# A recurrent mixer with a gated block: eight units' preparation laid over six columns, two of them in idle partitions and moved by transfers

## The chip, the cores and the metric

One core of one Trainium2 chip. The metric is the device time in microseconds (us) of one launch. Inputs are laid out on the host, all arithmetic is on the chip.

## The reference

A linear recurrence over 768 tokens for 4 batches of 8 heads with 40 features each, then a gated feed-forward block over the 4 batches. Cut to what matters:

```python
for t in range(S):
    y[:, :, t] = np.einsum('bhd,bhde->bhe', rt, state)
    Sa = np.einsum('bhde,bhe->bhd', state, at)
    state_decay = state * wt[:, :, None, :] - np.einsum('bhd,bhe->bhde', Sa, bt)
    state = state_decay + np.einsum('bhd,bhe->bhde', vt, kt)
# x = y of all heads side by side
h = np.maximum(x @ w_in, 0.0)
u, v = h[..., :512], h[..., 512:]
v_n = (v - mean(v)) / sqrt(var(v) + 1e-6)
v_s = np.einsum('ts,bsd->btd', w_spatial, v_n) + b_spatial[None, :, None]
out = (u * v_s) @ w_out
```

## The kernel before

**Layout.** `phase1` runs the recurrence in 24 chunks of 64 tokens (12 chunks for each of two pairs of batches). A chunk has 8 units (2 batches x 4 head pairs). A unit's two heads lie in the two halves of the 128 partitions (`par` 0 and 1). Of the 64 partitions of a half, 40 hold the head's features (E = 40); 24 hold padding. Tokens run along the free axis.

**Preparation** of a chunk q (needed some chunks later) is DVE's: `scan1` (L292) makes S, the products of the decay w from the end of the chunk backwards, and a reciprocal (L296); `scan2` (L301) makes Et, the forward products; `at_mul` (L318) and `sl_mul` (L324) make `at` (a times Et) and `sl` (b and k times S). The inputs of a chunk are one tile `ein` of 528 + 1536 elements per partition, two buffers, loaded by `prep_piece` (L279) in six transfers of 16 rows. `scr_store` (L312) sends the chunk's total decay out to memory, `scn_load` (L534) brings it back spread over the partitions. `lprime` (L339) makes the 32 x 32 diagonal blocks L' of the chunk's triangle on PE; `lblock` (L349) copies them with a mask into `Lc` on DVE. For every four chunks `invert` (L357 to L374) inverts the 32 x 32 triangles of `Lc` on DVE, in 30 steps of a product (L363) and a sum (L367) between transposes.

**The chunk loop** (chunk s) is a chain: `c_bp` (PE, L545; ACT copies it, L555), `c_ff` (L563; L571), `c_xx` (L581; L592), `c_mp` (L613, L619; DVE makes the state Mc, L630) and `c_y` (L641; DVE makes y, L654), then bp of s + 1. Beside it run the steps that make a later chunk's operands: `b_copy` (a copy of `at` into `At`, L392), `b_lka`, `b_h`, `b_tok`, `b_l21`, `b_zt`, `b_x21`, with copies on ACT and POOL's `strict` (L406). The feed-forward's first part (`m_*`) is woven in from chunk 11 on; `phase2` (L102) is the spatial product and the output projection.

**What sets the order.** Each engine, and SP's queue of transfers, does its instructions in program order. That order is the sorted list `plan`: `at(t, fn, ...)` gives each step a time t in units of chunks. `PREP` gives t of the preparation of a chunk q (scan1 at t + 0.20, the pieces of chunk q + 2 from t + 0.40, `lprime` at t + `LPO`), by default q - 8 + 0.01. All transfers but a few at the start are issued by SP.

Of the kernel before, what the change touches and what calls it, by code (L numbers as in the profile page):

```python
# [18 lines left out]
P = 128  # L19
C = 64  # L20
# [8 lines left out]
EW = WF + 3 * NU * C  # L29
NR = C + E  # L30
# [187 lines left out]
def phase1(ctx, tc, early, late, vtok, win, xs, vns, uts, dscr):  # L218
# [12 lines left out]
    fifo = [pool(f"fifo{i}") for i in range(GS)]  # L231
# [4 lines left out]
    etp = pool("etp", 9)  # L236
# [15 lines left out]
    ein = [p.tile([P, EW], F32, name=f"ein{i}") for i, p in enumerate((pin, pin, extra, extra))]  # L252
# [16 lines left out]

    def prep_load(s, rows, cols=slice(0, EW), i=None, queues=(nc.sync, nc.sync)):  # L270
        t = ein[s % 2 if i is None else i]
        for par in range(2):
            o = par * 64
            queues[par].dma_start(out=t[o:o + rows, cols], in_=early[par, s, 0:rows, cols])

    def prep_piece(s, k):
        par, r = k % 2, k // 2 * 16
        o = par * 64 + r
        nc.sync.dma_start(out=ein[s % 2][o:o + 16], in_=early[par, s, r:r + 16])  # L279

    def scan1(s, i=None):
        t = ein[s % 2 if i is None else i]
        Et = etp.tile([P, WF], F32, name="Et")
        at = fifo[s % 8].tile([P, NU, C], F32, name="at")
        sl = fifo[s % 8].tile([P, NU, 2, C], F32, name="sl")
        wseg = t[:, 0:WF]
        oth = t[:, WF:].rearrange("p (q n c) -> p n q c", q=3, c=C)
        sx = pin.tile([P, WF], F32, name="S", bufs=2)
        sv = sx.rearrange("p (n c) -> p n c", c=WSEG)
        st["pre", s] = (Et, at, sl)  # L290
        st["raw", s] = (wseg, oth, sv)
        nc.vector.tensor_tensor_scan(  # L292
            out=sx[:, ::-1], data0=wseg[:, ::-1], data1=ends[:, ::-1],
            initial=0.0, op0=ALU.mult, op1=ALU.add,
        )
        nc.vector.reciprocal(out=eseg[:, :, 0:1], in_=sv[:, :, 1:2])  # L296

    def scan2(s):
        Et, at, sl = st["pre", s]
        wseg, oth, sv = st["raw", s]  # L300
        nc.vector.tensor_tensor_scan(  # L301
            out=Et, data0=wseg, data1=ends, initial=0.0, op0=ALU.mult, op1=ALU.add,
        )
# [10 lines left out]
    def at_mul(s, eng, ns=slice(0, NU)):  # L314
        Et, at, sl = st["pre", s]
        oth = st["raw", s][1]
        Ev = Et.rearrange("p (n c) -> p n c", c=WSEG)
        eng.tensor_tensor(out=at[:, ns], in0=oth[:, ns, 0], in1=Ev[:, ns, 0:C], op=ALU.mult)  # L318

    def sl_mul(s, eng, ns=slice(0, NU)):  # L320
        Et, at, sl = st["pre", s]
        wseg, oth, sv = st["raw", s]
# [6 lines left out]
    def lprime(s, units=range(NU)):  # L329
# [4 lines left out]
        for n in units:  # L334
            for blk in range(2):
                for par in range(2):
# [3 lines left out]
                        pl[o:o + HB, n, :], lhsT=sl[PR[par], n, par, cs], rhs=at[PR[par], n, cs],  # L340
# [3 lines left out]
    def lblock(s):  # L344
        if s % GS == 0:
# [3 lines left out]
        nc.vector.tensor_tensor(  # L349
            out=Lc[:, u0:u0 + NU, :], in0=st.pop(("pl", s)),  # L350
            in1=maskl.unsqueeze(1).broadcast_to([P, NU, HB]), op=ALU.mult,
        )
# [33 lines left out]
    def b_copy(s, par):  # L386
        if par == 0:
            At = [jat.tile([P, NU, C], F32, name=f"At{i}") for i in range(2)]
            tk = jit.tile([P, NU, 2, E], F32, name="tk")
            st["blk", s] = (At, Rts[s % 2], tk, xfs[s % 2])  # L390
        at = st["pre", s][1]
        nc.sync.dma_start(out=st["blk", s][0][par][PR[par]], in_=at[PR[par]])  # L392
# [18 lines left out]
    def b_lka_out(s, par):  # L411
# [174 lines left out]
    def c_xx_out(s, g):  # L586
# [439 lines left out]
```

## Time and profile before

| | |
|---|---|
| median of 3 runs | 667.58 us (663.11 to 670.05) |
| profiled execution, its own time | 665.08 us |
| its span, first to last instruction | 663.3 us |
| mean granted TensorE clock | 0.943 |
| DVE busy | 448.4 us (68%) |
| PE busy | 571.8 us (86%) |
| ACT, POOL busy | 384.2 us, 225.9 us |
| transfers of SP's queue | 105672 packets, 84.31 MB |

The span is what the profile's tables cover; the execution's own time is 1.8 us more. Busy time leaves out waiting and the issue of transfers: SP's work is seen in its timeline alone. Stages differ, so busy time is read by windows. In a row of a timeline the bracket gives the idle time before it and what ended it; q behind an engine's name means its queue.

### The profile page before, as it was taken

How to read it: one execution, taken by the hardware profiler on the slowest of the kernel's cores; microseconds unless marked ns; L12 is line 12 of the kernel's file. 1: busy time of each engine (PE TensorE's matmuls, PEld its weight loads, DVE VectorE, ACT ScalarE, POOL GpSimd, SP SyncE). 2: the span in 40 equal slices, each digit the busy share in tenths (PEclk: the TensorE clock that was granted, in tenths of full speed). 3: DMA queues.
4: the chain of work that ended last, by engine and by line, in shares of the span. 5: the costliest groups of instructions: out<-in, count | busy, mean ns of one | idle time of the engine just before them, and what ended most of it. 6: DMA issues, size and time to landing. Idle time of an engine off the chain costs nothing.

```text
span 663.3 us, 25848 instructions
## 1 busy us (share of the span) xinstructions
PE 571.8 (86%) x10960; PEld 518.3 (78%) x10960; DVE 448.4 (68%) x970; ACT 384.2 (58%) x860; POOL 225.9 (34%) x298
## 2 busy tenths in 40 slices
PE   1447885498777887999999999999989999999997
PEld 1437674487766776888888888888878999999997
DVE  8999789989999999488896677343384842332220
ACT  2135662377666775688878887888765543221212
POOL 6013330224332334144341332332354843352221
PEclk9967997789787898999999999999998999999999
DMA  8654778477555546657565365375395557150001
GB/s 199 121 107 67 134 152 147 70 175 155 135 127 115 131 117 120 142 127 172 154 190 148 86 173 144 90 198 132 89 262 182 162 155 240 61 157 31 31 31 59
DMA packets 106331, 87.68 MB, mean 132 GB/s; under 512 B 35496, under 2 KB 92072, under 8 KB 104296
## 3 DMA queue, kind: packets, MB, share of 16 engines
q1 hardware_dynamic: 105672, 84.31, 52.0%
q10 hardware_dynamic: 544, 1.72, 1.2%
q8 instruction: 86, 1.41, 1.0%
q14 instruction: 29, 0.24, 0.1%
HBM read 59.20 MB, written 20.50 MB: 120 GB/s over the span
## 4 chain that ended last, share of the span: by engine, by line
PE 63%; DVE 15%; DMA 7%; issue 6%; ACT 4%; SPq 3%; POOL 1%; DVEq 0%; ACTq 0%; POOLq 0%
PE po L199 6%; PE pv L759 6%; PE pv L712 6%; PE pg L179 5%; PE pg L180 5%; PE pg L181 5%; PE ch L563 4%; PE bp L545 4%; PE ch L581 4%; PE bk L429 2%; DMA ein<-in_early 2%; DVE itmp L363 2%; PE bk L451 2%; PE bk L399 2%; PE bp L641 2%
## 5 line engine op out<-in xcount | busy, mean ns | idle before, releaser
L406 POOL TENSOR_SCALAR_AFFINE_SELECT Rt<-Rt 64x512 f32<-64x512 f32 (+1 forms) x144 | 83.8, 584 | 156.2 <-ACT Rt L592 128.5
L406 POOL TENSOR_SCALAR_AFFINE_SELECT At<-At 64x512 f32<-64x512 f32 x48 | 41.5, 864 | 164.0 <-ACT At L416 151.9
L555 ACT ACTIVATE Rt<-bp 64x416 f32<-64x416 f32 x96 | 49.1, 511 | 56.2 <-PE bp L545 53.6
L363 DVE TENSOR_TENSOR itmp<-A 128x30 f32<-128x30 f32 (+9 forms) x180 | 66.5, 369 | 3.4
L179 PE MATMUL pg<-wsh,vh 128*128 128x384 f32 x192 | 65.4, 341 | 2.0 <-ACT vh L51 2.0
L545 PE MATMUL bp<-lin,Mc 40*64 40x104 f32 x768 | 47.3, 278 | 22.1 <-DVE y L654 19.8
L183 DVE TENSOR_TENSOR g<-pg,bb 128x384 f32<-128x384 f32 x32 | 17.8, 556 | 70.7 <-PE pg L181 68.4
L180 PE MATMUL pg<-wsl,vh 128*128 128x384 f32 x192 | 65.1, 339 | 0.0
L181 PE MATMUL pg<-wsh,vl 128*128 128x384 f32 x192 | 63.6, 339 | 0.0
L367 DVE TENSOR_TENSOR A<-A,itmp 128x30 f32<-128x30 f32 (+9 forms) x180 | 59.1, 328 | 6.2
L545 PEld LDWEIGHTS bp<-lin,Mc 40*64 40x64 f32 x768 | 40.7, 150 | 25.5 <-DVE y L654 22.7
L563 PE MATMUL ch<-Rt,At 128*64 128x104 f32 x768 | 48.0, 283 | 5.9 <-issue 4.8
L55 POOL TENSOR_TENSOR gl<-g,gh 128x384 fp32r<-128x384 f32 x32 | 33.0, 1035 | 58.1 <-ACT gh L51 58.1
L592 ACT ACTIVATE Rt<-ch 64x416 f32<-64x416 f32 x96 | 49.1, 511 | 4.6 <-PE ch L581 2.2
L563 PEld LDWEIGHTS ch<-Rt,At 128*64 128x64 f32 x768 | 42.2, 157 | 10.4 <-issue 7.1
L51 ACT ACTIVATE gh<-g 128x384 fp32r<-128x384 f32 x32 | 16.7, 521 | 54.3 <-DVE g L184 54.3
L339 PE MATMUL bk<-at,sl 64*32 64x32 f32 x1536 | 21.2, 203 | 26.5 <-DVE sl L324 20.7
L55 POOL TENSOR_TENSOR vl<-raw,vh 128x512 fp32r<-128x512 f32 x24 | 31.5, 1324 | 31.6 <-ACT vh L51 30.1
L581 PE MATMUL ch<-ffs,xf 64*64 64x104 f32 x768 | 41.7, 261 | 0.0
L339 PEld LDWEIGHTS bk<-at,sl 64*32 64x32 f32 x1536 | 17.7, 114 | 29.5 <-issue 14.4
L179 PEld LDWEIGHTS pg<-wsh,vh 128*128 128x128 f32 x192 | 36.6, 190 | 2.4 <-ACT vh L51 2.2
L630 DVE TENSOR_TENSOR Mc<-ch,scn 104x160 f32<-104x160 f32 x44 | 18.5, 436 | 29.0 <-PE ch L619 18.7
(132 smaller groups left out, 1497.8 us busy)
## 6 DMA issues: line engine op xcount, KB each, us to landing
ein<-in_early SPq DMA_DIRECT2D x108, 129.0 KB
lin<-in_late SPq DMA_DIRECT2D x48, 160.0 KB
At<-at SPq DMA_DIRECT2D x48, 128.0 KB
uts<-ur SPq DMA_DIRECT2D x48, 128.0 KB
vns<-vr SPq DMA_DIRECT2D x24, 256.0 KB
raw<-vns SPq DMA_DIRECT2D x24, 256.0 KB
ut<-uts SPq DMA_DIRECT2D x24, 256.0 KB
Rt<-in_vtok SPq DMA_DIRECT2D x48, 80.0 KB
```

What stands on the lines that cost most here:

```text
L55: eng.tensor_tensor(out=lo, in0=x, in1=hi.bitcast(F32), op=ALU.subtract)
L179: nc.tensor.matmul(pg, lhsT=vh[:, dc], rhs=w_h, start=(i == 0), stop=False)
L180: nc.tensor.matmul(pg, lhsT=vh[:, dc], rhs=w_l, start=False, stop=False)
L181: nc.tensor.matmul(pg, lhsT=vl[:, dc], rhs=w_h, start=False, stop=(i == NT - 1))
L363: nc.vector.tensor_tensor(out=tp, in0=A[:, k + 1:, k:k + 1].broadcast_to([P, m, k]), in1=A[:, k:k + 1, 0:k].broadcast_to([P, m, k]), op=AL ...
L367: nc.vector.tensor_tensor(out=A[:, k + 1:, 0:k], in0=A[:, k + 1:, 0:k], in1=tp, op=ALU.add)
L406: nc.gpsimd.affine_select(out=t, in_=t, pattern=[[0, k], [1, C]], base=0, channel_multiplier=-1, compare_op=ALU.is_gt, fill=0.0,)
L545: nc.tensor.matmul(bp[PR[par], q, :], lhsT=Mc[RR[par], n, :], rhs=li[RR[par], n, C:], start=(q == 0), stop=False, skip_group_check=True,)
L555: nc.scalar.activation(Rt[par][PR[par], gp, :], st["bp", g][PR[par]], AF.Copy)
L563: nc.tensor.matmul(ff[PR[1 - par], q, :], lhsT=At[par][:, n, :], rhs=Rt[par][:, n, :], start=True, stop=True,)
L581: nc.tensor.matmul(xx[ev, q, :], lhsT=xf[ev, n, :], rhs=ffs[ev, q, :], start=True, stop=True,)
L592: done = nc.scalar.activation(Rt[par][PR[par], gp], xx[PR[1 - par]], AF.Copy, scale=-1.0)
```

## The change

From chunk 4 on, units 6 and 7 are prepared in the 24 idle partitions of each half, as extra rows of units 0 to 3: rows 0 to 23 of both go beside units 0 and 1, rows 24 to 39 beside units 2 and 3. The preparation's instructions then run over 6 columns (396, 384 and 768 elements) instead of 8 (528, 512, 1024). `ein` is filled by ten transfers a chunk. When `sl` is made, `relay` moves the results of the packed rows to where units 6 and 7 are expected, in eight transfers from SBUF to SBUF. `at`, `sl` and `Et` of a chunk now lie in one tile `pre`, of which there are nine. The total decay is copied into a spare column of Et, so that the relay carries it too.

Chunks 0 to 3 keep eight columns, in buffers `nat` of their own; the pieces of chunks 4 and 5 are issued at the start. Products on PE read 40 rows instead of 64. `lblock` becomes a copy by ACT without mask; POOL zeroes the upper triangles in `invert`. Branches that were not in use (`LKA_POOL`, `H_POOL`, `TRI_POOL`) go. Some due times are new: `PREP`, `LPQ` (L' of chunks 5 to 7), `INV_T`, `T_DEC`, the time of `scr_store`. The diff, cut to its core:

```diff
+NM = 6
+WM = NM * WSEG
+PW = WM + 3 * NM * C
...
     def prep_piece(s, k):
-        par, r = k % 2, k // 2 * 16
-        o = par * 64 + r
-        nc.sync.dma_start(out=ein[s % 2][o:o + 16], in_=early[par, s, r:r + 16])
+        par, k = k % 2, k // 2
+        o = par * 64
...
+        if k == 0:
+            nc.sync.dma_start(out=tw[o:o + E], in_=w[0:E, 0:WM])
+        elif k == 1:
+            nc.sync.dma_start(out=to[o:o + E], in_=oth[0:E, :, 0:NM * C])
+        elif k == 2:
+            m = 2 * WSEG
+            nc.sync.dma_start(
+                out=tw[o + E:o + C, 0:2 * m].rearrange("p (k x) -> p k x", k=2),
+                in_=w[0:48, WM:].rearrange("(k r) x -> r k x", k=2),
+            )
+        else:
+            m, r = 2 * C, 24 * (k - 3)
+            nc.sync.dma_start(
+                out=to[o + E:o + C, :, (k - 3) * m:(k - 2) * m], in_=oth[r:r + 24, :, NM * C:]
+            )
...
+    def relay(s):
+        for t, m in halves(s):
+            for par in range(2):
+                o = par * 64
+                nc.sync.dma_start(out=t[o:o + 24, NM * m:], in_=t[o + E:o + C, 0:2 * m])
+                nc.sync.dma_start(out=t[o + 24:o + E, NM * m:], in_=t[o + E:o + E + 16, 2 * m:4 * m])
...
         nc.vector.tensor_tensor_scan(
-            out=Et, data0=wseg, data1=ends, initial=0.0, op0=ALU.mult, op1=ALU.add,
+            out=halves(s)[1][0][:, 0:n * WSEG], data0=wseg, data1=ends[:, 0:n * WSEG],
+            initial=0.0, op0=ALU.mult, op1=ALU.add,
         )
+        if s >= GS:
+            nc.vector.tensor_copy(out=Et[:, 0:n, C + 1], in_=sv[:, 0:n, 1])
...
-                        pl[o:o + HB, n, :], lhsT=sl[PR[par], n, par, cs], rhs=at[PR[par], n, cs],
+                        pl[o:o + HB, n, :], lhsT=sl[RR[par], n, par, cs], rhs=at[RR[par], n, cs],
...
+        else:
+            nc.scalar.activation(Lc[:, u0:u0 + NU, :], st.pop(("pl", s)), AF.Copy, scale=-1.0)
...
+        h = HB // 2 if g else 0
+        while h:
+            x = Af.rearrange("p (b x) -> p b x", x=2 * h * (HB + 1))[:, :, h:h + h * HB]
+            nc.gpsimd.memset(x.rearrange("p b (r c) -> p b r c", c=HB)[:, :, :, 0:h], 0.0)
+            h //= 2
...
-    PREP = {4: 0.03, 5: 0.45, 6: 1.03, 7: 1.45, 8: 2.03, 9: 2.45, 10: 3.03, 11: 3.45}
+    LPQ = {5: 0.89, 6: 0.9, 7: 0.8}
+    INV_T = {1: (2.3, 3.74), 2: (4.5, 7.6), 3: (8.0, 11.7), 4: (12.0, 15.74), 5: (16.0, 19.7)}
...
+        at(RLY.get(q, max(t + 0.36, OV.get((sl_mul, q), 0) + 0.005)), relay, q)
         if q + 2 < NS:
-            gap = 0.03 if q < 8 else 0.07 if q < 12 else 0.14
-            for k in range(6):
-                at(t + 0.40 + gap * k, prep_piece, q + 2, k)
-        at(t + LPO, lprime, q)
-        at(t + LPO + 0.05, lblock, q)
+            gap = GAP.get(q, 0.07 if q < 12 else 0.14)
+            for k in range(10):
+                at(max(t + 0.40, OV.get((sl_mul, q), 0) + 0.01) + gap * k, prep_piece, q + 2, k)
+        at(t + LPQ.get(q, LPO), lprime, q)
+        at(t + LPQ.get(q, LPO) + 0.05, lblock, q)
```

**SP's queue, chunk 0.** After `scn_load` of chunk 0 and the copies `At` of chunk 1, before:

```order
L392 DMA At_611<-at 64x512
L381 DMA lin_136<-in_late 40x8x128 x2
L279 DMA ein_120<-in_early 16x2064 x6
L312 DMA scr<-sc 40x8 x4
L279 DMA ein_121<-in_early 16x2064 x6
L534 DMA scn<-scr 64x320 x2
```

and now (the first relay, of chunk 4, then the pieces of chunk 6; the next relay, of chunk 5, is left out but for its first row):

```order
L441 DMA At_136<-pre_70 40x8x64
L431 DMA lin_141<-in_late 40x8x128 x2
L313 DMA pre_582<-pre_582 24x384
L314 DMA pre_582<-pre_582 16x384
...
L290 DMA ein_125<-in_early 40x396 x2
L292 DMA ein_125<-in_early 40x3x384 x2
L295 DMA ein_125<-in_early 24x2x132 x2
L301 DMA ein_125<-in_early 24x3x128 x4
L313 DMA pre_588<-pre_588 24x384
...
L571 DMA scn<-scr 64x320 x2
```

Between lin and the next scn load stood 16 transfers; now there are 37, among them two relays of eight.

**PE, the end of chunk 4.** `L380` is L' of chunk 12, from the tile `pre` that its relay fills; ahead of it stands y of chunk 4, behind it bp of chunk 5:

```order
L668 MATMUL bp_2567<-Rt_139,tk 40x64
L668 MATMUL bp_2567<-Rt_140,tk 40x64
L380 MATMUL bk<-pre_582 32x32 x32
L582 MATMUL bp_2896<-lin_141,Mc 64x104 x8
L582 MATMUL bp_2914<-lin_141,Mc 64x104 x8
L448 MATMUL bk<-pre_600 64x64 x16
```

The place in PE's queue is the old one; what L380 reads now comes through transfers. L' of chunk 7 stood behind ff of chunk 2 and stands ahead of it now.

**DVE, chunk 2.** L402 is the first transpose of the inverse of chunks 4 to 7, the other rows prepare chunk 8. Before, the whole preparation stood ahead of the transpose:

```order
L292 SCALAR_TENSOR_TENSOR S<-ein_120,ends 128x528
L296 RECIPROCAL ends<-S 128x8
L301 SCALAR_TENSOR_TENSOR Et<-ein_120,ends 128x528
L318 TENSOR_TENSOR at<-ein_120,Et 128x512
L324 TENSOR_TENSOR sl<-ein_120,S 128x1024
L349 TENSOR_TENSOR Lc<-bk,maskl 128x256
L357 STREAM_TRANSPOSE A<-Lc 128x1024
```

and now:

```order
L328 SCALAR_TENSOR_TENSOR S<-ein_125,ends 128x396
L332 RECIPROCAL ends<-S 128x6
L402 STREAM_TRANSPOSE A<-Lc 128x1024
L338 SCALAR_TENSOR_TENSOR pre_606<-ein_125,ends 128x396
L343 COPY pre_606<-S 128x6
L358 TENSOR_TENSOR pre_606<-ein_125,pre_606 128x6x64
L365 TENSOR_TENSOR pre_606<-ein_125,S 128x6x128
```

The transpose moved ahead of all but the first scan, and the masked copy (L349) has left DVE.

More of the change, by code (lines that the diff above doesn't have):

```diff
@@ L29 @@
 EW = WF + 3 * NU * C
+NM = 6
+WM = NM * WSEG
+PW = WM + 3 * NM * C
+TW = 3 * C
+NT9 = 9
 NR = C + E
@@ L230, in phase1 @@
     pin = pool("pin")
-    fifo = [pool(f"fifo{i}") for i in range(GS)]
+    fifo = [pool(f"fifo{i}").tile([P, NU * TW + WF], F32, name=f"pre{i}") for i in range(GS)]
     inv = pool("inv")
@@ L251, in phase1 @@
     extra = early_bufs.enter_context(tc.tile_pool(name="extra", bufs=1, side="right"))
-    ein = [p.tile([P, EW], F32, name=f"ein{i}") for i, p in enumerate((pin, pin, extra, extra))]
+    nat = [extra.tile([P, EW], F32, name=f"nat{i}") for i in range(GS)]
+    ein = [pin.tile([P, PW], F32, name=f"ein{i}") for i in range(2)]
     ends = pin.tile([P, WF], F32, name="ends")
@@ L267, in phase1, with units, prep_load @@
     st, marks = {}, {}
-    def prep_load(s, rows, cols=slice(0, EW), i=None, queues=(nc.sync, nc.sync)):
-        t = ein[s % 2 if i is None else i]
+    def units(s):
+        return NU if s < GS else NM
+    def prep_load(s, rows, cols=slice(0, EW), queues=(nc.sync, nc.sync)):
         for par in range(2):
             o = par * 64
-            queues[par].dma_start(out=t[o:o + rows, cols], in_=early[par, s, 0:rows, cols])
+            queues[par].dma_start(out=nat[s][o:o + rows, cols], in_=early[par, s, 0:rows, cols])
@@ new lines, in halves, with scan1 @@
+    def halves(s):
+        t = fifo[s % NT9]
+        return (t[:, 0:NU * TW], TW), (t[:, NU * TW:], WSEG)
+    def relay(s):
[4 more added lines that the diff above has]
+                nc.sync.dma_start(out=t[o + 24:o + E, NM * m:], in_=t[o + E:o + E + 16, 2 * m:4 * m])
+    def scan1(s):
+        n = units(s)
+        t = nat[s] if s < GS else ein[s % 2]
+        ops, Et = (x.rearrange("p (n c) -> p n c", c=m) for x, m in halves(s))
+        wseg = t[:, 0:n * WSEG]
+        oth = t[:, n * WSEG:].rearrange("p (q n c) -> p n q c", q=3, c=C)
@@ L897, in phase1 @@
             )
-        pads(p, ein[2])
-        pads(p, ein[3])
+        pads(p, nat[2])
+        pads(p, nat[3])
+        for t in ein:
+            p.memset(t[:, 4 * WSEG:WM], 1.0)
+            p.memset(t[:, WM:], 0.0)
         for q, cols in ((0, W), (1, W), (0, O), (1, O), (2, W), (2, O), (3, W), (3, O)):
-            prep_load(q, 48 if q else 64, cols, q, qs)
+            prep_load(q, 48 if q else 64, cols, qs)
         for par in range(2):
@@ L904, in phase1 @@
             vtok_load(0, par)
+        for q in (4, 5):
+            for k in range(10):
+                prep_piece(q, k)
         make_identity(nc, ident)
[L906 to L913 removed]
+        for t in (Mc, *xfs, *Ats[0], *Ats[1]):
             p.memset(t, 0.0)
```

148 lines of the change are left out of this document (60 added, 88 removed).

## The prediction

> **What bounds the kernel now.** I read the page's sums first, then the busy time by stage, then the timelines of DVE and of SP's queue, because the change takes work from DVE and hands transfers to SP.
>
> ```profile
> PE 571.8 (86%) x10960; PEld 518.3 (78%) x10960; DVE 448.4 (68%) x970; ACT 384.2 (58%) x860; POOL 225.9 (34%) x298
> PE   1447885498777887999999999999989999999997
> DVE  8999789989999999488896677343384842332220
> core 0: us, PE busy (x) PEld busy (x) DVE busy (x) ACT busy (x) POOL busy (x), PEclk, DMA share, GB/s
> 54.00:134.00 80.00, 56.05 (x1678) 48.84 (x1674) 70.19 (x127) 42.01 (x99) 24.51 (x30) 0.86 0.67 119
> 134.00:255.00 121.00, 101.20 (x2896) 89.55 (x2896) 114.61 (x229) 86.38 (x195) 39.49 (x57) 0.90 0.59 135
> 278.00:350.00 72.00, 71.56 (x1683) 62.50 (x1683) 63.06 (x143) 57.24 (x134) 27.34 (x38) 1.00 0.62 159
> ```
>
> PE leads the average, but the stages differ. From 134 to 255 us DVE works 114.61 of 121 us: it is the bound there. From 278 to 350 us PE works 71.56 of 72 us, and a faster DVE buys nothing. The rows below say which chunk is where: y of chunk 3 ends at 134.2, of chunk 4 at 151.8, of chunk 9 at 241.8, of chunk 11 at 277.8, of chunk 15 at 350.5.
>
> ```profile
> 54.00 1.23 DVE L292 TENSOR_TENSOR_SCAN S<-ein,ends 128x528 f32<-128x528 f32 x1
> 57.42 1.22 DVE L324 TENSOR_TENSOR sl<-ein,S 128x1024 f32<-128x1024 f32 x1
> ...
> 66.63 1.26 DVE L292 TENSOR_TENSOR_SCAN S<-ein,ends 128x528 f32<-128x528 f32 x1 [0.58 <-DMA ein<-in_early]
> ...
> 84.63 1.26 DVE L292 TENSOR_TENSOR_SCAN S<-ein,ends 128x528 f32<-128x528 f32 x1 [0.96 <-DMA scr<-sc]
> ...
> 133.44 0.75 DVE L654 TENSOR_TENSOR y<-bp,Et 104x256 f32<-104x256 f32 x2
> 151.35 0.42 DVE L654 TENSOR_TENSOR y<-bp,Et 104x256 f32<-104x256 f32 x1
> 241.00 0.75 DVE L654 TENSOR_TENSOR y<-bp,Et 104x256 f32<-104x256 f32 x2
> 277.38 0.42 DVE L654 TENSOR_TENSOR y<-bp,Et 104x256 f32<-104x256 f32 x1 [0.78 <-PE bp L641]
> 349.71 0.80 DVE L654 TENSOR_TENSOR y<-bp,Et 104x256 f32<-104x256 f32 x2
> ```
>
> SP's own timeline shows a second thing that the busy sums leave out. Its columns are start, length of the merged stretch, and the transfers in it.
>
> ```profile
> 58.66 3.19 SPq L279 DMA_DIRECT2D ein<-in_early  x6
> 61.95 1.56 SPq L312 DMA_DIRECT2D scr<-sc  x4
> 63.95 4.37 SPq L279 DMA_DIRECT2D ein<-in_early  x6
> 68.36 1.16 SPq L534 DMA_DIRECT2D scn<-scr  x2
> ...
> 82.15 0.87 SPq L312 DMA_DIRECT2D scr<-sc  x2
> 83.12 2.35 SPq L279 DMA_DIRECT2D ein<-in_early  x4
> 85.57 1.57 SPq L666 DMA_DIRECT2D xs<-y  x4
> ...
> 109.59 0.41 SPq L60 DMA_DIRECT2D d_raw<-in_win  x1
> 114.34 0.67 SPq L312 DMA_DIRECT2D scr<-sc  x2
> ```
>
> From 58.66 to 110.0 us SP issues one transfer behind the other; its first real pause is the one from 110.0 to 114.34. In that stretch SP is as full as DVE.
>
> **What the change takes from DVE.** These groups (count, busy us, mean ns) are the preparation.
>
> ```profile
> L301 DVE TENSOR_TENSOR_SCAN Et<-ein,ends 128x528 f32<-128x528 f32 x24 | 34.0, 1417 | 0.5
> L292 DVE TENSOR_TENSOR_SCAN S<-ein,ends 128x528 f32<-128x528 f32 x24 | 30.1, 1253 | 2.3 <-DMA ein<-in_early 1.2 <-DMA scr<-sc 1.0
> L318 DVE TENSOR_TENSOR at<-ein,Et 128x512 f32<-128x512 f32 x24 | 19.8, 827 | 2.0 <-DMA ein<-in_early 1.2
> L349 DVE TENSOR_TENSOR Lc<-bk,maskl 128x256 f32<-128x256 f32 x24 | 10.1, 419 | 5.5 <-PE bk L339 5.5
> L296 DVE RECIPROCAL ends<-S 128x8 f32<-128x8 f32 x24 | 4.9, 206 | 0.8
> ```
>
> For chunks 4 to 23 the four long ones run over six units instead of eight, so each loses a quarter: 0.35 + 0.31 + 0.21, and 0.30 of sl's 1.22, together 1.17 us. The masked copy of the triangle, 0.42 us, goes to ACT, which is busy 86.38 of 121 us in the DVE stage and takes it beside other work; were ACT full it would cost the chain about as much as DVE paid. A new copy of six elements per row is bounded by nothing and the 0.21 us of the reciprocal on eight; I take 0.15. Net 1.44 us a chunk, 20 times, 29 us of DVE work; about 15 of these chunks are prepared before 255 us, so 22 us could show if nothing else came in. PE's products over 40 rows instead of 64 keep their columns, and I cost that at nothing. POOL zeroes triangles of the inverse, 16 to 256 elements each; DVE has the rest of a chunk's preparation between, and POOL idles two thirds of the stage.
>
> **What it adds to SP.** Per chunk 10 pieces instead of 6, and 8 relays, so 18 issues where there were 6. The price of an issue comes from these rows (minimum/median/maximum ns).
>
> ```profile
> L279 SPq DMA_DIRECT2D ein<-in_early x108: 320/444/1912, 58.7 to 323.7; - x108
> L312 SPq DMA_DIRECT2D scr<-sc x44: 273/322/790, 22.0 to 339.2; - x44
> L666 SPq DMA_DIRECT2D xs<-y x48: 273/355/964, 85.6 to 492.7; - x48
> L392 SPq DMA_DIRECT2D At<-at x48: 477/540/1864, 17.6 to 461.3; - x48
> L381 SPq DMA_DIRECT2D lin<-in_late x48: 798/844/1309, 12.6 to 445.5; - x48
> L384 SPq DMA_DIRECT2D Rt<-in_vtok x48: 557/594/1542, 13.6 to 466.1; - x48
> L534 SPq DMA_DIRECT2D scn<-scr x44: 450/594/1837, 34.6 to 459.2; - x44
> L60 SPq DMA_DIRECT2D d_raw<-in_win x6: 367/368/1577, 109.6 to 213.8; - x6
> ```
>
> The four stores of 40 rows at 85.57 took 1.57 us, 0.39 each with the pause between two issues, about 0.04. The new transfers have 16, 24 or 40 rows. Below they are bounded by the stores of scr (0.322 + 0.04), above by the copy At from SBUF to SBUF with 64 rows (0.540 + 0.05 = 0.59). The nearest in rows are the stores, 0.39, and the 16-row loads, 0.444 + 0.045 = 0.49; I take 0.44, the middle. A chunk then costs SP 7.9 us in place of 6 x 0.49 = 2.9.
>
> The Trainium skill says otherwise: "DMA: Bandwidth & Descriptors", section "Issuing engines are not separate DMA queues", calls the sequencer's time to initiate a DMA usually small relative to the DMA itself. By that rule SP would be no bound and the sum would be the faster rival below; the 51 us in which SP does nothing but issue speak against it here.
>
> **The head, chunks 0 to 4.** In the new program SP has 198 transfers between the first relay of chunk 4 and the first relay of chunk 12: 64 relays, 80 pieces and 54 others. The others, by medians: scr 14 x 0.322, scn 8 x 0.594, At 8 x 0.540, lin 8 x 0.844, xs 8 x 0.355, vtok 6 x 0.594, weights 2 x 0.368, that is 27.4 us, and 54 pauses of 0.045 make 29.9. The 144 new ones at 0.44 make 63.4. The first relay waits for sl of chunk 4: that ended at 58.6 and now ends 0.95 us earlier (its share of the quarters, less the copy), at 57.7. So chunk 12's relay starts at 57.7 + 93.3 = 151.0, is issued by 154.5, and lands some time later. The landing is bounded by the scr stores (issued by 83.0, DVE released at 84.6: 1.6 us) and by the pieces (issued by 61.9, DVE released at 66.6: 4.8 us); a relay is small like the stores, I take 2.2. PE's order holds the rest:
>
> ```profile
> 151.21 1.38 PE L545 MATMUL bp<-lin,Mc 40*64 40x104 f32 x26
> ```
>
> The block product of chunk 12 stands in PE's queue just ahead of bp of chunk 5, and so now waits for the relay: 154.5 + 2.2 + 0.7 for the product is 157.4, where bp of chunk 5 began at 151.2. **The head costs 6 us**, although DVE alone, with eight chunks of 1.44 us less, would have been done at about 140. Queued behind that waiting product is the whole chain of the chunk: bp, ff, xx, y.
>
> Within the head the same happens earlier. The block product of chunk 7 now stands ahead of ff of chunk 2 and waits for its relay, and DVE's transposes of the first inverse come ahead of the rest of chunk 8's preparation; DVE idles there, which eats the time that it was given.
>
> **Chunks 5 to 9.** SP's others per chunk: At 2 x 0.585, scn 2 x 0.64, lin 2 x 0.89, vtok 2 x 0.64, scr 2 x 0.37, a weight 0.41, xs 1.6 every second chunk: 7.5 on average; with 7.9 it is 15.4 us. DVE: 114.61 over the seven chunks 4 to 10 is 16.4, now 14.9. A chunk took 121 / 7 = 17.3, 0.9 more than DVE's work. Two queues in order, each at 15 and each waiting for the other once a chunk (relay for sl, scan for pieces), will not overlap better; I take SP's 15.4 + 0.8 = 16.2. Gain 1.1 x 5 = **5.5 us**.
>
> **Chunks 10 and 11** also load the first xt (12 transfers, 7.2 us) and three stores: SP comes to 37.1 us by the same prices, where the two chunks took 277.8 - 241.8 = 36.0. Loss **1 us**. **Chunks 12 to 15**: SP 17.4 a chunk, PE 18 with no idle time. SP fits under PE on paper, but a relay that is late stops PE's whole queue; bounds 0 and 5, I take **3 us**. From chunk 16 on there are no preparations and PE's work is as before.
>
> **Sum**, against the profiled execution's 665.1 (span 663.3 and 1.8 around it; the median of three is 667.6): 665.1 + 6 - 5.5 + 1 + 3 = 669.6, **forecast 669**. Inside this case, with the issue price between 0.42 and 0.455, 661 to 676. 340 relays and pieces lie on the line that counts, so 0.01 us of price is about 3.4 us of time: the price decides.
>
> **Rival, faster.** Issues cost what the scr stores do, 0.37. The head's 144 save 10.1 us, bp of chunk 5 starts near 147.4; DVE sets the chunks 5 to 10 at 14.9 + 0.9 = 15.8, 1.5 less than before, six times; chunks 10 and 11 gain about 1.5 more at SP; nothing is lost later. 665.1 - 3.8 - 9 - 1.5 = 651. For it: rows of 40 are among the cheapest issues. Against: no load into SBUF has a median under 0.368. The skill's rule named above would lead here.
>
> **Rival, slower.** Issues cost the 0.49 of today's 16-row loads, or stall as those do at up to 1.9 us when too many are in flight. From 0.455 the loss passes 1%; at 0.49 it is 669.6 + 5 x 3.4 = 686. For it: it is the very line that the change multiplies, and a copy from SBUF to SBUF costs 0.59 today. Against: those loads have rows of 8 KB, the new ones 0.5 to 1.6 KB, which should land sooner.
>
> **A third**, that the change's gain is simply hidden, fails on the head: the profile there has no cover, since SP was already full.
>
> **Chances.** The forecast's case 0.37, the faster rival 0.32, the slower 0.31. Within 1% (about what a measurement of this kernel can tell from no change) I give 0.31, nearly all from the first case, whose edges send 0.02 to faster and 0.04 to slower: faster 0.34, slower 0.35. The range takes in both rivals' times, 651 to 688.
>
> **What would show it.** Right: SP without a pause from about 58 to beyond 150; new PE idle time just before L' (the block product, released by a transfer); chunk 5 starting 4 to 8 us later than 151; DVE's busy sum down by 25 to 31 us with more idle time; scans at 0.95 us. Wrong on price: a median issue of pieces or relays under 0.40 or over 0.48. Wrong altogether: SP with pauses of several us in the first six chunks, or chunks 5 to 9 at 17 us with SP idle.

## The result, and the profile after

The changed kernel takes **742.1 us** (median of 4 runs, 739.2 to 742.9) where the kernel before takes 666.8 (4 runs, 663.1 to 670.1): 1.114 times as long, 95% interval 1.110 to 1.119. The forecast was 669, its range 651 to 688. The direction that held is the slower rival's, with about four times its loss. In the experiments further down some executions came out slower at a lower granted clock; a time is the median of all executions of a kernel, a ratio leaves these out.

The page of the changed kernel, its busy sums, two of its rows of slices, and the chain that ended last:

```profile
span 741.1 us, 26185 instructions
PE 607.6 (82%) x10960; PEld 547.4 (74%) x10960; DVE 414.5 (56%) x970; ACT 395.2 (53%) x880; POOL 221.3 (30%) x335
PE   1478665665786768797979999999998999999997
DVE  8995349756398766737664745664445353233221
PE 51%; SPq 18%; DMA 12%; DVE 10%; ACT 4%; issue 4%; DVEq 0%; POOL 0%; ACTq 0%
SPq L313 6%; PE po L204 6%; PE ch L600 5%; SPq L314 4%; PE pv L786 4%; PE pg L184 4%; PE pv L739 4%; PE pg L185 4%; PE pg L186 4%; PE ch L618 4%; DMA Rt<-in_vtok 3%; DMA ein<-in_early 3%; PE bk L488 3%; DVE itmp L413 2%; DVE A L417 2%
```

DVE's sum has fallen by 33.9 us (448.4 to 414.5), where 29 were forecast. Yet the kernel is 78 us longer (spans, 663.3 to 741.1). The chain says where: SP's queue holds 18% of it, and the two relay lines, L313 and L314, head the list of SP's part. The same stages as the prediction showed, by chunk (chunks 1 to 3, 4 to 10, 12 to 15):

```profile
core 0: us, PE busy (x) PEld busy (x) DVE busy (x) ACT busy (x) POOL busy (x), PEclk, DMA share, GB/s
54.00:153.00 99.00, 64.84 (x1652) 56.54 (x1646) 60.40 (x128) 43.68 (x103) 18.53 (x35) 0.71 0.34 88
153.00:308.00 155.00, 112.80 (x2896) 98.63 (x2896) 103.60 (x229) 91.57 (x205) 37.93 (x67) 0.79 0.43 110
334.00:426.00 92.00, 80.66 (x1738) 70.30 (x1729) 58.74 (x145) 60.38 (x139) 26.81 (x43) 0.91 0.42 115
```

Nothing that this table counts is full any more: DVE works 103.60 of 155 us where it worked 114.61 of 121, PE 80.66 of 92 where it had no idle time. The DMA engines are at 0.34 to 0.43 where they were at 0.59 to 0.67, so it isn't the moving of the data either. PE's busy time alone misleads here: in chunks 4 to 10 it grew from 101.20 to 112.80 us for the same 2896 products, with the granted clock at 0.79 where it was 0.90. What is full is a queue that the table leaves out. SP's own timeline, with start, length and transfers, from the first relay on:

```profile
57.81 0.79 SPq L313 DMA_DIRECT2D pre<-pre  x1
58.65 0.61 SPq L314 DMA_DIRECT2D pre<-pre  x1
...
62.92 0.56 SPq L314 DMA_DIRECT2D pre<-pre  x1
63.92 0.69 SPq L290 DMA_DIRECT2D ein<-in_early  x2
64.66 0.79 SPq L292 DMA_DIRECT2D ein<-in_early  x2
...
66.31 1.61 SPq L301 DMA_DIRECT2D ein<-in_early  x4
68.12 0.90 SPq L313 DMA_DIRECT2D pre<-pre  x1
...
81.97 1.80 SPq L441 DMA_DIRECT2D At<-pre  x2
83.88 0.79 SPq L431 DMA_DIRECT2D lin<-in_late  x1
84.77 0.78 SPq L313 DMA_DIRECT2D pre<-pre  x1
```

The relays of one chunk take from 57.81 to 63.48, 5.7 us. Summed over the whole stretch from there to the end of y of chunk 15 (426.2), SP issues for 327 us, spends 30 us in the short pauses between two issues, and has 11 us of longer pauses in all, none over 1.6. In the same stretch of the kernel before (57.8 to 350.5) it issued for 208 us and had 65 us of longer pauses. The prices, minimum/median/maximum ns:

```profile
L313 SPq DMA_DIRECT2D pre<-pre x80: 728/742/1431, 57.8 to 422.3; - x80
L314 SPq DMA_DIRECT2D pre<-pre x80: 519/555/1376, 58.7 to 423.0; - x80
L290 SPq DMA_DIRECT2D ein<-in_early x40: 292/336/1509, 17.8 to 382.1; - x40
L301 SPq DMA_DIRECT2D ein<-in_early x80: 298/371/1900, 22.3 to 388.3; - x80
L441 SPq DMA_DIRECT2D At<-pre x48: 811/844/903, 29.3 to 537.5; - x48
```

A relay of 24 rows costs SP 0.742, one of 16 rows 0.555, a piece about 0.35. The copy At, which now reads 40 rows in eight parts out of the shared tile, went from 0.540 to 0.844. The waits that this makes, and the ends of y (chunks 3, 4, 9, 11, 15):

```profile
PE bk L380 <- DMA pre<-pre: 39.4, 16, 7.8
DVE Mc L657 <- PE ch L646: 37.0, 24, 8.7
PE ch L600 <- DMA Rt<-in_vtok: 33.1, 16, 5.1
152.19 0.78 DVE L681 TENSOR_TENSOR y<-bp,pre 104x256 f32<-104x256 f32 x2
180.41 0.41 DVE L681 TENSOR_TENSOR y<-bp,pre 104x256 f32<-104x256 f32 x1
289.93 0.74 DVE L681 TENSOR_TENSOR y<-bp,pre 104x256 f32<-104x256 f32 x2
333.65 0.42 DVE L681 TENSOR_TENSOR y<-bp,pre 104x256 f32<-104x256 f32 x1 [0.78 <-PE bp L668]
425.74 0.42 DVE L681 TENSOR_TENSOR y<-bp,pre 104x256 f32<-104x256 f32 x1 [0.78 <-PE bp L668]
```

PE waits for the relay ahead of the triangle's product (L380), and nearly as long, ahead of ff (L600), for vtok, a load that the change did not touch and that only stands behind the relays in SP's queue. y of chunk 3 ends at 153.0 (before 134.2), of chunk 9 at 290.7 (241.8), of chunk 15 at 426.2 (350.5). From there to the end both kernels take about the same, 315 and 313 us.

### The profile page after: what moved, and what is told of

The parts are those of the page before. It is cut to its first block, busy times and chain, and to the rows that moved or that the text cites. A ratio compares the mean times of both kernels' runs of the same rounds, so it can differ in the third digit from the quotient of the medians.

```text
span 741.1 us, 26185 instructions
## 1 busy us (share of the span) xinstructions
PE 607.6 (82%) x10960; PEld 547.4 (74%) x10960; DVE 414.5 (56%) x970; ACT 395.2 (53%) x880; POOL 221.3 (30%) x335
## 4 chain that ended last, share of the span: by engine, by line
PE 51%; SPq 18%; DMA 12%; DVE 10%; ACT 4%; issue 4%; DVEq 0%; POOL 0%; ACTq 0%
SPq L313 6%; PE po L204 6%; PE ch L600 5%; SPq L314 4%; PE pv L786 4%; PE pg L184 4%; PE pv L739 4%; PE pg L185 4%; PE pg L186 4%; PE ch L618 4%; DMA Rt<-in_vtok 3%; DMA ein<-in_early 3%; PE bk L488 3%; DVE itmp L413 2%; DVE A L417 2%
## 5 line engine op out<-in xcount | busy, mean ns | idle before, releaser
L455 POOL TENSOR_SCALAR_AFFINE_SELECT Rt<-Rt 64x512 f32<-64x512 f32 (+1 forms) x144 | 76.3, 530 | 202.8 <-ACT Rt L628 160.6
L600 PE MATMUL ch<-Rt,At 128*64 128x104 f32 x768 | 63.5, 323 | 42.1 <-DMA Rt<-in_vtok 33.1
L600 PEld LDWEIGHTS ch<-Rt,At 128*64 128x64 f32 x768 | 54.2, 183 | 49.3 <-issue 34.9
L455 POOL TENSOR_SCALAR_AFFINE_SELECT At<-At 64x512 f32<-64x512 f32 x48 | 37.6, 783 | 169.4 <-ACT At L464 167.9
L380 PE MATMUL bk<-pre 40*32 40x32 f32 x1536 | 27.9, 211 | 60.8 <-DMA pre<-pre 39.4
L380 PEld LDWEIGHTS bk<-pre 40*32 40x32 f32 x1536 | 22.9, 121 | 65.5 <-DMA pre<-pre 38.3
L413 DVE TENSOR_TENSOR itmp<-A 128x30 f32<-128x30 f32 (+9 forms) x180 | 63.3, 352 | 3.4
L186 PE MATMUL pg<-wsh,vl 128*128 128x384 f32 x192 | 61.8, 336 | 0.0
L608 ACT ACTIVATE ffs<-ch 128x416 f32<-128x416 f32 x48 | 24.1, 514 | 52.0 <-PE ch L600 51.9
L60 POOL TENSOR_TENSOR gl<-g,gh 128x384 fp32r<-128x384 f32 x32 | 32.5, 1024 | 60.4 <-ACT gh L56 60.4
L747 DVE BATCH_NORM_STATS2 bs<-vr 128x6 f32<-128x512 f32 x24 | 16.6, 690 | 50.1 <-ACT vr L741 50.1
```

The lines of the kernel that those rows point to most:

```text
L60: eng.tensor_tensor(out=lo, in0=x, in1=hi.bitcast(F32), op=ALU.subtract)
L186: nc.tensor.matmul(pg, lhsT=vl[:, dc], rhs=w_h, start=False, stop=(i == NT - 1))
L380: nc.tensor.matmul(pl[o:o + HB, n, :], lhsT=sl[RR[par], n, par, cs], rhs=at[RR[par], n, cs], start=True, stop=True,)
L413: nc.vector.tensor_tensor(out=tp, in0=A[:, k + 1:, k:k + 1].broadcast_to([P, m, k]), in1=A[:, k:k + 1, 0:k].broadcast_to([P, m, k]), op=AL ...
L455: nc.gpsimd.affine_select(out=t, in_=t, pattern=[[0, k], [1, C]], base=0, channel_multiplier=-1, compare_op=ALU.is_gt, fill=0.0,)
L600: nc.tensor.matmul(ff[PR[1 - par], q, :], lhsT=At[par][:, n, :], rhs=Rt[par][:, n, :], start=True, stop=True,)
```

## The experiments

Three theories stood at the start. **A**: SP's issue time. The relays fill SP's queue, and every transfer behind them is late, whoever waits for it. **B**: the landing. The triangle's product waits for the relay's data. **C**: the rest of the change (ScalarE's copy of the triangle, GpSimd's zeroing, the new order) costs the time.

### No relay at all

```
     def relay(s):
-        for t, m in halves(s):
...
+        return
```

> The change without its relays: the results of units 6 and 7 of chunks 4 to 23 are never moved to their place, so these two units are computed from zeros. Theory A (SP's issue time): the 160 relays hold SP for about 0.73 us each, 117 us in all; without them SP has 12.7 us of work a chunk and is no longer the bound, DVE's shorter work shows: 640 to 660 us, SP with pauses of several us per chunk. Theory B (the landing that the block product L' waits for): the same, 640 to 660, since that wait goes too. Theory C (the ACT copy of the triangle, POOL's zeroing or the new due times cost the time): it stays above 720.

Measured 658.2 us, ratio to before 0.992 (0.988 to 0.996). C falls: with all the rest of the change in place the kernel is a little faster than before. It also gives the most that the six-unit form can bring in this order of steps, 0.8%, with its relay for nothing. What the run leaves out is the move: units 6 and 7 of chunks 4 to 23 are then computed from zeros, but in chunks 9 to 12 and 18 to 21 from what chunks 0 to 3 left in the same one of the nine tiles. The same holds for the other runs whose relay is missing or unread.

### The same relays, read by nobody

```
+    spare = const.tile([P, 2 * TW], F32, name="spare")
...
-                nc.sync.dma_start(out=t[o:o + 24, NM * m:], in_=t[o + E:o + C, 0:2 * m])
+            nc.sync.dma_start(out=spare[o:o + 24], in_=t[o + E:o + C, 0:2 * m])
...
```

> The relays are issued as in the change, same forms and same place in SP's queue, same wait for sl, but into a spare tile that nobody reads; units 6 and 7 of chunks 4 to 23 are computed from zeros as in the run without relays. Theory A (issue time): nearly as slow as the change, 720 to 742 us, since SP is as full; the gain is at most the 2 to 3 us of a landing where SP was ahead. Theory B (landing): as fast as without relays, 640 to 660, since no product waits for them.

Measured 740.6 us (two executions), ratio 1.117 (1.107 to 1.128), as slow as the changed kernel, with nobody waiting for a relay. B falls as the cause of the 78 us, and A stands: it is enough that SP issues them.

### The relays on another engine's queue

```
-                nc.sync.dma_start(out=t[o:o + 24, NM * m:], in_=t[o + E:o + C, 0:2 * m])
+                nc.gpsimd.dma_start(out=t[o:o + 24, NM * m:], in_=t[o + E:o + C, 0:2 * m])
...
```

and the same with nc.scalar.

> The same eight relays issued by POOL instead of SP. Theory A: SP's queue is freed as without relays, and POOL (5 us busy a chunk) takes eight issues; at 0.6 to 1.3 us each POOL has 10 to 15 us a chunk, less than a chunk lasts, but its triangles for the chain (ff, mp, y wait for them) come later: 655 to 700 us. Theory B (landing): the products wait for the same landings, 725 to 745 us.

> The same eight relays issued by ACT instead of SP. Theory A: SP is freed, but ACT, with 12 to 14 us of work a chunk in the chain, gets 5.9 us of issues at SP's price and stands still whenever sl is not ready: 18 to 20 us a chunk to chunk 15, 670 to 710 us. Theory B (landing): 725 to 745 us.

On GpSimd 674.2 us, ratio 1.007 (1.003 to 1.012): some 70 us of the loss are gone by the choice of the queue alone. On ScalarE 834.7 (two executions), ratio 1.259, far outside what was expected. The relay's row on GpSimd, its row on ScalarE, ScalarE's longest wait in all, and one case of it from ScalarE's timeline:

```profile
L313 POOL DMA_DIRECT2D pre<-pre x80: 516/516/686, 58.4 to 348.1; - x80
```

```profile
L313 ACTq DMA_DIRECT2D pre<-pre x80: 772/773/1887, 58.0 to 505.5; - x80
```

```profile
ACT ffs L608 <- DMA pre<-pre: 137.7, 13, 13.6
178.08 0.51 ACT L608 ACTIVATE ffs<-ch 128x416 f32<-128x416 f32 x1
178.45 0.77 ACTq L313 DMA_DIRECT2D pre<-pre  x1
...
187.04 0.54 ACTq L314 DMA_DIRECT2D pre<-pre  x1
187.63 0.52 ACT L608 ACTIVATE ffs<-ch 128x416 f32<-128x416 f32 x1 [9.04 <-DMA pre<-pre]
```

ScalarE pays about SP's price for the issue (0.773), and its own work stands behind the eight relays: between the two ffs shown (its copies of ff) it issues for 5.6 us and stands between the issues for 3.5. Such waits of ffs come to 137.7 us, in 13 places. GpSimd pays 0.516, less than the 0.6 to 1.3 us that were assumed for it without a row, and its queue has time for it.

The Trainium skill's page "DMA: Bandwidth & Descriptors", section "Issuing engines are not separate DMA queues", says that issuing from several engines saves only the sequencer's time to initiate a transfer, usually small beside the transfer. What it saves is what it says; here that was not small, some 70 us of 742.

### Fewer pieces, and what a large load costs

The input of chunks 4 to 23 is laid out on the host as the six-unit form needs it, so that one transfer of 64 rows replaces five pieces.

```
-    def prep_piece(s, k):
...
+    def prep_piece(s, par):
+        o = par * 64
+        nc.sync.dma_start(out=ein[s % 2][o:o + 64], in_=early[par, s, :, 0:PW])
```

> The input of chunks 4 to 23 is laid out for the six-unit form on the host (layout only, no arithmetic), so that a chunk's load is 2 transfers of 64 rows instead of 10 pieces; the 8 relays of a chunk stay on SyncE. Theory A (SyncE's issue time sets the stages up to chunk 15): ten pieces cost SyncE about 10 x 0.41 = 4.1 us a chunk with their pauses, two large loads about 1.0; 18 chunks x 3.1 = 56 us of SyncE time less, and the unread relays had cost about 82 us of time for 110 us of SyncE, so 0.75 x 56 = 42 us less: 695 to 710. Theory B (what is waited for is the pieces' data itself, their landing): the same bytes and more land no sooner, 735 to 745.

> The kernel without relays (units 6 and 7 of chunks 4 to 23 computed from zeros) with the packed loads in place of its ten pieces. If SyncE's issue time were all that counts, 56 us of it less would leave it at the floor of the run without relays or a little under: 652 to 660. If the packed loads cost something of their own (396 KB in one transfer, for whose landing SyncE was seen waiting at the transfer 8 places on), they cost it here too: 664 to 675, and the 16 us that the packed runs with relays on GpSimd lost against this are theirs in part.

With the relays on SP 700.6 us, ratio 1.054 (1.051 to 1.057): eight issues less a chunk, 42 us, as A said. Without any relay, the packed loads gave 666.8, ratio 1.001 (0.997 to 1.005), against 0.992 with ten pieces. So where SP is no longer the bound, the large loads cost about 1% themselves. In the run through DRAM below, SP was seen standing for the landing of such a load, issued eight transfers back (at 83.8 and 85.8 us); no run took that wait alone away.

### The price list

> The kernel without relays (units 6 and 7 of chunks 4 to 23 are computed from zeros), and behind its end a list of transfers of one form each, twice, on SyncE, ScalarE and GpSimd in turn: SBUF to SBUF with 8 to 64 rows of 1536 B, DRAM to SBUF and SBUF to DRAM with 16, 24 and 40 rows, and the copy of 40 and 64 rows in 8 parts of 256 B. Its time says nothing; the issue's duration on the engine is read from the trace. Theory A1 (the price goes by whether both ends are in SBUF): 24 rows SBUF to SBUF near 0.73 and 16 rows near 0.54 on SyncE, the same rows to or from DRAM near 0.3. Theory A2 (the price goes by the number of rows alone): 24 rows cost 0.73 in all three directions. On GpSimd 0.51 whatever the form; on ScalarE 0.77 and 0.54 as in the run with the relays there.

Single transfers on SP behind the end of the kernel, from its timeline; the list runs twice, and the rows are of the second pass. The first six are from SBUF to SBUF with 8, 24, 32, 40, 48 and 64 rows of 1536 B, the next fence has 16 rows (L77), then DRAM:

```profile
667.74 0.72 SPq L75 DMA_DIRECT2D pb<-pa  x1
669.39 0.75 SPq L75 DMA_DIRECT2D pb<-pa  x1
671.93 0.54 SPq L75 DMA_DIRECT2D pb<-pa  x1
672.51 0.75 SPq L75 DMA_DIRECT2D pb<-pa  x1
673.30 0.54 SPq L75 DMA_DIRECT2D pb<-pa  x1
673.89 0.60 SPq L75 DMA_DIRECT2D pb<-pa  x1
```

```profile
675.63 0.53 SPq L77 DMA_DIRECT2D pb<-pa  x1
679.12 0.29 SPq L79 DMA_DIRECT2D pb<-pd  x1
682.17 0.29 SPq L80 DMA_DIRECT2D pe<-pa  x1
682.52 0.32 SPq L79 DMA_DIRECT2D pb<-pd  x1
684.51 0.89 SPq L81 DMA_DIRECT2D pb<-pa  x1
```

The price does not rise with the rows: 32 and 48 rows cost 0.54, 24 and 40 cost 0.75. The same 24 rows cost 0.29 when one end is in DRAM, in either direction (L79 a load, L80 a store; the load of 40 rows 0.32); in the list's first pass the store took 0.29 again, but the load 0.54, and the load of 16 rows 0.58. L81 is the copy At's new form, 40 rows in eight parts: 0.89. The rows of 16 are the least even: 0.53 twice in L77, but 0.755 and 1.364 in L75, where they stood second in the list. A1 holds for 24 and 40 rows, A2 falls.

### A third more rows, a lower price

```
-            nc.sync.dma_start(out=spare[o:o + 24], in_=t[o + E:o + C, 0:2 * m])
+            nc.sync.dma_start(out=spare[o:o + 32], in_=t[o + 32:o + C, 0:2 * m - 24])
...
```

(96 B less a row in two of the forms, for want of room.)

> As the run whose 8 relays of a chunk go to a spare tile that nobody reads (units 6 and 7 of chunks 4 to 23 computed from zeros), but the four of 24 rows carry 32 rows each: a third more rows and bytes, the same number of transfers. Theory A1' (a transfer from SBUF to SBUF costs SyncE 0.53 us where its rows are a multiple of 16 and 0.75 where they are not, as in the list of single forms): 4 x 0.20 us less a chunk, 16 us of SyncE, at 0.75 about 12 us less than the 741 there: 722 to 734. Rival (the price grows with rows or bytes, and the list's 0.75 was something else): 740 to 750.

The price fell as the list says. The row of the run with 24 rows, then that with 32:

```profile
L314 SPq DMA_DIRECT2D spare<-pre x40: 728/784/2137, 58.0 to 415.8; - x40
```

```profile
L315 SPq DMA_DIRECT2D spare<-pre x40: 535/582/624, 57.8 to 410.0; - x40
```

The time did not fall as far: 739.0 us, ratio 1.110 (1.104 to 1.116) against 1.117 (1.107 to 1.128), 5 us by the ratios where 12 were expected, and the intervals overlap. That the price changed is shown; that the time followed is not.

### The relay through DRAM, and the loads on GpSimd

Four stores of 24 rows, and 0.15 of a chunk later four loads of 40 rows, replace the eight from SBUF to SBUF, on top of the packed loads.

```
+                nc.sync.dma_start(
+                    out=rly[m][s, par].rearrange("(k r) x -> r k x", k=2),
+                    in_=t[o + E:o + C, 0:4 * m].rearrange("p (k x) -> p k x", k=2),
+                )
+
+    def relay_in(s):
...
+                nc.sync.dma_start(out=t[o:o + E, NM * m:], in_=rly[m][s, par, 0:E])
```

Two more runs let GpSimd issue the packed loads, with the relay through DRAM and with the direct one:

```
-        nc.sync.dma_start(out=ein[s % 2][o:o + 64], in_=early[par, s, :, 0:PW])
+        nc.gpsimd.dma_start(out=ein[s % 2][o:o + 64], in_=early[par, s, :, 0:PW])
```

> As the run with packed loads, and the relay of a chunk goes through DRAM: 4 stores of 24 rows, then, 0.15 of a chunk later, 4 loads of 40 rows, in place of 8 transfers from SBUF to SBUF. Theory A (SyncE's issue time): in the list of single forms a store of 24 rows took 0.29 us and a load of 40 rows 0.32 to 0.33, so a chunk's relay takes SyncE 4 x 0.29 + 4 x 0.33 + 8 x 0.045 = 2.8 us, where the eight from SBUF to SBUF took 2.57 x 2 + 0.36 = 5.5; 20 x 2.7 = 54 us of SyncE less, at 0.75 a further 40 us, so about 660, no lower than the 658 without any relay: 655 to 672. Rival D (two landings, one behind the other, about 2.2 us each, and loads that wait at the head of SyncE's queue for the stores): no better than the packed loads alone, 690 to 705.

> As the run with packed loads and the relay through DRAM, but GpSimd issues the two packed loads of a chunk, 0.12 of a chunk later; SyncE keeps the relay's 4 stores and 4 loads. With the loads on SyncE the trace showed SyncE waiting for the landing of a packed load that stood 8 transfers back (at 83.8 and 85.8 us), so theory A with that wait added: SyncE issues 2.8 us a chunk where the run without relays issued 4.1 for its pieces, GpSimd 2 x 0.55: as fast as without relays but for the relay's own landing, 655 to 670. Rival D (what the packed run with DRAM lost was the relay's landing, for which TensorE waited 18 us in 13 places): no better than 683, 676 to 690.

> As the run with packed loads, its 8 relays of a chunk from SBUF to SBUF on SyncE, but GpSimd issues the two packed loads of a chunk, 0.12 of a chunk later. Theory A: SyncE issues 5.5 us a chunk for the relays and no piece, 1.4 more than the 4.1 of the run without relays, and no lane is held by a packed load: 28 us of SyncE more than that run, at up to 0.75 some 10 to 21 us on its 658: 665 to 682. Rival D (a landing on the way to the triangle costs what is left): like the packed loads alone with the load's wait taken off, 690 or more.

Through DRAM 683.6 us, ratio 1.029 (1.023 to 1.035), between the two expectations. The loads cost what the list said (median 0.331), the stores, which have two parts a row here, a little more (0.370 for 0.29), and SP now has 56 us of longer pauses in 306. What is left is told by PE's wait:

```profile
PE bk L370 <- DMA pre<-rly: 18.3, 13, 2.7
```

The product of the triangle waits for the relay 13 times. Without a relay this product began 5.2 to 8.0 us after the end of sl in chunks 13 to 17; with the relay through DRAM its last load is issued 4.7 to 6.0 us after the end of sl (the two that the product needs stand two ahead), and lands later still. Here B is back: once SP is relieved, the way of the data itself is longer than what the order had left for it.

With the loads on GpSimd as well, the relay through DRAM got worse, 697.9 us, ratio 1.046 (1.040 to 1.053). The direct relay got better, 690.5, ratio 1.035 (1.028 to 1.043) against 1.054 with the loads on SP, but stayed above the 665 to 682 of A. A's number for the first, 655 to 670, is refuted: SP had 84 us of longer pauses in it, and time was lost all the same. GpSimd's queue stood at these loads, and PE's wait for the relay grew:

```profile
POOL ein L285 <- DVE pre L355: 34.7, 7, 17.7
PE bk L370 <- DMA pre<-rly: 24.0, 16, 3.5
```

### Unread relays on GpSimd, and the relay shared

```
-            nc.sync.dma_start(out=spare[o:o + 24], in_=t[o + E:o + C, 0:2 * m])
+            nc.gpsimd.dma_start(out=spare[o:o + 24], in_=t[o + E:o + C, 0:2 * m])
...
```

> GpSimd issues eight relays a chunk into a spare tile that nobody reads (units 6 and 7 of chunks 4 to 23 computed from zeros), the ten pieces stay on SyncE. Nobody waits for these landings, so what it loses against the 658 without relays is GpSimd's time and its waits for VectorE's products at the head of its queue: if that is what the run with the real relays on GpSimd (674) lost, 669 to 677; if it was the landing ahead of the triangle, 656 to 663.

> As the run with packed loads on SyncE, but the relay is shared: GpSimd issues the four transfers that the triangle waits for (at and sl), SyncE the four of Et. SyncE per chunk: two loads 1.0 + four relays 2.6 + pauses, about 3.9, a little under the 4.1 of the run without relays; GpSimd 4 x 0.52 = 2.1 where the run with all eight there had 4.2 and lost 16 us against the run without. Half of that: 658 + 8 = 666; 660 to 673. If what that run lost was not GpSimd's time but the relay's landing, no better than its 674: 672 to 680.

> As the run with packed loads on SyncE, and all eight relays of a chunk issued by GpSimd. SyncE is then left with two loads a chunk, 3 us less than in the run with the relays on GpSimd and ten pieces on SyncE (674). If SyncE no longer set the pace there, as its theory says, this brings little: 668 to 677. If SyncE's pieces still cost it time, down to 660 to 667.

Unread on GpSimd: 662.4 us, ratio 0.995 (0.992 to 0.998). Against no relay at all (0.992) GpSimd's issuing costs at most little; against the relays that are read (1.007) some 1.2% hang on somebody reading them. That agrees with the landing as the second cost, about 8 us. Where in the chunk they are lost isn't shown: on GpSimd the trace has PE waiting for a relay for less than 1 us in all.

With packed loads, the shared relay gave 674.7, ratio 1.016 (1.010 to 1.021), and all relays on GpSimd 680.6, ratio 1.023 (1.016 to 1.029). Neither fell under the 1.007 of the ten pieces: what the packed loads cost by themselves (1%) is in both. The first falls into the 672 to 680 that was set down for the landing, the second lies above its 668 to 677.

### ScalarE's copy alone, in the kernel before

```
+        if s < GS:
...
+        else:
+            nc.scalar.activation(Lc[:, u0:u0 + NU, :], st.pop(("pl", s)), AF.Copy, scale=-1.0)
```

with the zeroing in the inversion.

> The kernel before with one part of the change alone: from chunk 4 on ScalarE copies the triangle's blocks (scale -1) and GpSimd zeroes the upper parts in the inversion; no relay, no six-unit form. VectorE is freed of 0.42 us a chunk; chunks 4 to 9, where it is busy 97%, would give 6 x 0.42 = 2.5 us: 660 to 666, ratio 0.992 to 1.002. Theory C (this part costs: ScalarE's copy comes late, or the zeroing stands in the inversion's way): ratio above 1.01.

664.8 us, ratio 0.997 (0.994 to 1.001). The 2.5 us that were expected would be 0.4%; no difference is shown, and no loss either. No version whose relay is read was faster than the kernel before.

## Why the prediction was wrong

**What bounds the kernel, and the balance.** Right. The prediction said that SP does nothing but issue from 58 us on, that the change multiplies this line, and that the price decides. Most signs it named for that came: SP without a pause far beyond 150 us (none over 1.6 us up to 426), PE idle ahead of the triangle's product, released by a transfer (39.4 us), DVE's sum down, a little further than said (33.9 us for 25 to 31), scans near 0.95 (median 0.98). Chunk 5 came 36 us late instead of 4 to 8, and the sign for a wrong price came too: the relays' medians lie over 0.48, the pieces' under 0.40.

**The step that failed is the price of an issue**: bounded "above by the copy At from SBUF to SBUF with 64 rows (0.540 + 0.05 = 0.59)", and "I take 0.44, the middle" of the rows nearest in size. The relay cost 0.742 and 0.555 by the medians, 0.70 on average with its long ones, and with the pause 0.75. It lies outside both bounds. The nearest row in kind, SBUF to SBUF, was At alone, and its 64 rows looked like an upper bound for 24; the list shows that 24 rows are dearer than 64 (0.75 and 0.60). The pieces came out as forecast, 0.43 + 0.045 on average. In the prediction's own terms, for the 340 new issues between the first relay and the end of chunk 15: 160 relays took 119.6 us with their pauses where 160 x 0.44 = 70.4 were taken, 49 more; 180 pieces 85.6 for 79.2, 6 more. Medians also hide the long issues: the relays' mean is 0.70 and the pieces' 0.43, and the 16-row loads of the kernel before, priced at their median of 0.444, had a mean of 0.60.

**At was costed as unchanged.** Its part of the diff, from one tile's 64 rows to 40 rows in eight parts, was read and not priced: 30 copies at 0.86 in place of 0.62 (their means before and after in this stretch) are 7 us.

**The balance closes with that.** Of the 327 us of issuing, 112 are relays and 77 pieces; the other 137, less the 7 that At has gained, are 130, and their pauses 15. With 340 x 0.44 = 150 for the new ones SP would have needed 295 us for a stretch that was 293 us long before: hence a forecast of about no change. 295 + 49 + 6 + 7 is 357, and with the 11 us of longer pauses 368, which is the length that the stretch has.

**The head**: forecast 6 us at bp of chunk 5 (157.4 for 151.2), measured 36 there (186.9), of which 29 had come by the end of y of chunk 4 (151.8 to 180.8). The mechanism, the product of chunk 12 ahead of bp of chunk 5, was right, only the relay that it waits for started at 181.8 and not at 151.0:

```profile
181.76 0.80 SPq L313 DMA_DIRECT2D pre<-pre  x1
186.19 0.79 PE L380 MATMUL bk<-pre 40*32 40x32 f32 x16 [7.83 <-DMA pre<-pre]
186.91 2.52 PE L582 MATMUL bp<-lin,Mc 40*64 40x104 f32 x26
```

The product stopped ahead of its last 16 of 64 matmuls, those of units 6 and 7.

**Chunks 5 to 9**: a gain of 5.5 forecast, a loss of 20 measured from the end of y of chunk 4 (90.0 us before, 109.8 after), some 7 of it the wait just shown. The gain is there as soon as SP is out of the way: without relays these chunks took 83.4 us, 6.6 less. So DVE's term was well sized, and of "two queues in order, each at 15" only DVE was. **Chunks 10 and 11**: 7 for 1. **Chunks 12 to 15**: 19 for 3. There "SP fits under PE on paper" was 17.4 us a chunk; at the real price it is SP that sets the chunk, 23.0 us (92.1 / 4), above PE's 18.

**The slope** of 3.4 us for 0.01 of price was a fair guide where SP is full. A change of the mean price from 0.44 to 0.60 (relays and pieces with their pauses) gives 56 us by it; the median rose by 73 over the forecast, the rest being At and the pauses. The range didn't follow from the prediction's own bounds: at the upper one, 0.59, the slope gives 669.6 + 15 x 3.4 = 721, and the range ended at 688.

**The rivals.** The faster one needed an issue at 0.37: only the medians of the pieces came near it (0.336 to 0.371 without the pause). The slower one named the right cause but stopped at 0.49, the price of a load, and so at 686, though it named the 0.59 of At. That long issues come from too many transfers in flight, as it says, no run here settled.

**What stays open.** Without relays the stretch after chunk 15 is 5 us longer than before (658.7 - 340.9 against 663.3 - 350.5), so that of the 9.7 us won by then less than 5 are left at the end; no run looked into that. Nor did a run ask whether the left-out data of units 6 and 7 change the time by themselves, or how much the lower granted clock adds to the loss. Nor is it settled how the 8 us between read and unread relays on GpSimd divide.

## What to carry to other kernels

An engine that only issues transfers is a resource with a sum of its own, in no busy column: add up its issues over a stage, compare with the stage's length, and if they are near, price each added transfer from a row of the same kind (both ends, form), not of the nearest size. Freeing the busiest engine by transfers pays only if the queue they go to has room: here the same eight transfers a chunk, read by nobody, cost some 83 us on SP and some 2 on GpSimd (by the ratios, 1.117 and 0.995 against 0.992). And when a queue is relieved, look at once for the landing behind it.

## What the runs showed of the hardware

- The issue of a single transfer from SBUF to SBUF took SP 0.52 to 0.60 us with 32, 48 or 64 rows (16 rows: 0.53, but 0.755 and 1.364 as well) and 0.72 to 0.79 with 8, 24 or 40; to or from DRAM 16, 24 and 40 rows took 0.27 to 0.35 in nine of twelve, 0.40 to 0.58 in the others. In the changed kernel a relay of 24 rows cost at least 0.728 with 1536 B a row and with 528 B. The Trainium skill, "DMA: Bandwidth & Descriptors", section "Why a DMA increments its semaphore by 16 and not by 1", says that such a transfer is spread over the largest number up to 16 that divides its outer dimension, and that the issuing sequencer itself writes the missing increments. By that rule 8, 24 and 40 rows would be the ones with extra work at the issue, as the list has it; but 24 rows to or from DRAM show no such step, so the rule alone doesn't explain the price.
- On GpSimd an issue took 0.49 to 0.55 us in nearly every form and direction (0.70 to 0.79 for the copies in eight parts); on ScalarE SBUF to SBUF cost about what it did on SP (24 and 40 rows 0.76 to 0.81, 32 rows 0.54).
- A transfer of 396 KB (64 rows of 6192 B) cost SP 0.59 to issue (median of the run without relays), and two of them in place of ten pieces still slowed the kernel by about 1% where SP had time.
